# Attention in 64x64 tiles: the masked quadrant of the scores left out, the keys' halves swapped for half of the heads, and a tile's work in an order with two changes of tiling

## The chip, the cores and the metric

The kernel runs on one core of a Trainium2 chip. The metric is the device time of one execution in microseconds (us). The kernel before takes 419.59 us (median of three runs, 418.76 to 420.72).

The engines are named as the profile names them: PE is TensorE (PEld its weight loads), DVE is VectorE, ACT is ScalarE, POOL is GpSimd, SP is SyncE, which here only issues transfers. Each engine works through its own instructions in order. A matmul of 32-bit floats is one instruction in the program and two in the trace ("x16" in a row of the trace is eight in the code).

## What is computed

A linear attention with decay over 2 batches, 8 heads, 768 positions and 64 numbers a head, and behind it two layers of a mixture of experts with one expert a row (1536 rows of 512, 8 experts, hidden size 1024):

```python
for t in range(S):
    state = gamma[None, :, None, None] * state + np.einsum('bhd,bhe->bhde', k[:, :, t], v[:, :, t])
    y[:, :, t] = scale * np.einsum('bhd,bhde->bhe', q[:, :, t], state)
x = np.ascontiguousarray(attn_out.transpose(0, 2, 1, 3)).reshape(B * S, H * D)
x = _moe_ref(x=x, **moe_kwargs)      # out[mask] = gate_w * (relu(xe @ w1[e]) @ w2[e])
return _moe2_ref(x=x, **moe2_kwargs) # the same with a capacity of 384 rows an expert
```

The change touches only the attention and what follows it up to the rows and gate logits of its 12 tiles.

## The kernel before

The attention (lines 476 to 733) goes over 12 tiles of 128 positions, n = 2 c + b for chunk c of batch b, one tile in one turn of the loop at line 662. Inside a tile the recurrence is written as matmuls, with all 8 heads in two halves j and four pairs p:

- `a_load` (485): SP issues the tile's q, k (both transposed) and v with k by rows, 1 MB, three tiles ahead.
- `a_decay` (498): POOL multiplies v by the decay, giving `vp`, one tile ahead.
- `a_scores` (506): PE forms `sc`, keys by queries, 128 by 128 for each head with 64 rows of the array (the profile's 64\*128 tiling: two matmuls lie side by side); DVE multiplies by the causal mask into `Am` (515), one instruction for each half of the heads.
- `a_state` (518): PE forms `du`, the tile's addition to the state (128\*64 tiling), DVE adds it to the state (`wn`, 532), POOL decays it (`wm`, 534). The last two tiles have none.
- `a_past` (538): PE starts the output `ot` with the old state times q (64\*64 tiling: four matmuls side by side).
- `a_out` (551): PE adds `vp` times `Am` to `ot` (128\*64 tiling); DVE scales it into `xt` (562), one instruction for each half of the heads.
- `a_comb` (574, with `combine`, 1347): PE turns `xt` back to rows and forms the gate logits in one go, `cb` (128\*128 tiling); DVE sums the logits (`lgb`, 1358, or into `row` from tile 8 on), then ACT copies the rows out of PSUM (1363), for tiles 0 to 7 the logits too (1367), and issues the store of the rows to DRAM, `x1d` (569).

The order is written out by hand (`manual_schedule`), and a turn stands on PE as: scores of n, `cb` of n-2, past of n-1, state of n, out of n-1. That makes four changes of tiling a turn. The PSUM buffers of all these are five of one tag (`mmtile`), and `cb` has one of its own.

Between the tiles stands the routing of rows to experts: tiles 0 to 3 and 4 to 7 are routed as batches (`batch`, 582: pick, count at n = 5 and 9; rank, slots, place at n = 6 to 8 and 10), tiles 8 to 11 one by one (`route_tile`, 196: pick, rank, place). At n = 6 `choose` (387) picks the expert that goes first and at n = 10 `early` (419) starts the gather of its rows. At n = 0 ACT makes the matrices `iw` from the identity and the gate's weights (692, 693), at n = 10 it casts two of the first weights (`split_hi`, 158, line 163). The tail behind the loop (711 to 740) does the last tile in two halves, `ca` and `cb` of `Halves` (1371), with the routing of tiles 9 to 11 between them, and then the first products of layer 1 begin.

Of the kernel before, what the change touches and what calls it, by code (L numbers as in the profile page):

```python
# [10 lines left out]
F32 = mybir.dt.float32  # L11
# [7 lines left out]
P = 128  # L19
B, H, S, HD = 2, 8, 768, 64  # L20
# [23 lines left out]
_C = {}  # L44


def _consts(capacity):
# [10 lines left out]
    put("mask", (s[:, None] <= s[None, :]))  # L58
    put("dec", gamma[None, :] ** (127.0 - s[:, None]))
    hh = np.array([[2 * p + j for p in range(NP)] for j in range(2)]).repeat(HD, axis=0)  # L60
# [22 lines left out]
def fused(ctx, tc, qT, kT, vkr, wg, w11, w12, w21, w22, cst, out, capacity):  # L83
# [12 lines left out]
    def mmtile(name):  # L96
        return pp.tile([P, 512], F32, tag="mm", name=name, bufs=5)

    cs = cp.tile([P, cst.shape[1]], F32, name="cs")
    c0, c1 = _C["g128"][1], _C["ident"][1]  # L100

    def con(name):
        lo, hi = _C[name]
        return cs[:, lo:hi]

# [369 lines left out]
    over = cp.tile([P, 2], F32, name="over")  # L475
    with tc.tile_pool(name="ap", bufs=3) as ap:
        W = []
        for b in range(B):
# [19 lines left out]
        def a_decay(n):  # L498
            if n >= NT:
                return  # L500
            vp = ap.tile([P, H, HD], F32, tag="vp", name="vp", bufs=3)
            dlo, dhi = _C["dec"]
            (V if n == 1 else G).tensor_mul(vp, ld[n][3], cs[:, dlo:dhi].unsqueeze(2).to_broadcast([P, H, HD]))
            vps[n] = vp

        def a_scores(n):
            qb, kt, k_, v_ = ld[n]
            Am = ap.tile([P, NP, 2, P], F32, tag="Am", name="Am", bufs=2)
            sc = [mmtile("sc").rearrange("p (a t) -> p a t", t=P) for _ in range(2)]
            for p in range(NP):  # L510
                for j in range(2):
                    hs = slice(j * HD, (j + 1) * HD)
                    T.matmul(sc[j][:, p, :], kt[hs, p, :], qb[hs, p, :], start=True, stop=True)  # L513
            for j in range(2):
                V.tensor_mul(Am[:, :, j, :], sc[j], con("mask").unsqueeze(1).to_broadcast([P, NP, P]))
            st_[n] = (vps.pop(n), Am)
# [33 lines left out]

        def a_out(n, beside=None):
            c, b = divmod(n, B)
            vp, Am = st_.pop(n)
            ot = st_.pop(("o", n))
            xt = ap.tile([P, NP, P], F32, tag="xt", name="xt", bufs=2)
            for j in range(2):
                for a in range(2):
                    for u in range(2):
                        p = 2 * a + u
                        T.matmul(ot[j][u * HD:(u + 1) * HD, a, :], vp[:, 2 * p + j, :], Am[:, p, j, :], start=not c,  # L560
                                 stop=True, skip_group_check=True)
                V.tensor_mul(xt[:, 2 * j:2 * j + 2], ot[j],
                             con("g").rearrange("p (k t) -> p k t", k=KD)[:, 2 * j:2 * j + 2])
                if beside is not None:
                    beside(j, xt[:, 2 * j:2 * j + 2])
            st_[("x", n)] = xt

        def a_store(n, row, cols=slice(0, RW)):
            nc.scalar.dma_start(x1d[n * P:(n + 1) * P, cols], row[:, cols])

        tlo, _ = _C["tok"]
        lgb = ap.tile([P, nb, E], F32, name="lgb", bufs=1)

        def a_comb(n):
            row, lg = combine(nc, pp, rp, st_.pop(("x", n)), iw[0], None, P, lgb[:, n, :] if n < nb else None)
            a_store(n, row)
            return lg

        def a_route(n, lg):
            return route_tile(rt1, lg, cs[:, tlo + n:tlo + n + 1], None, P, n == NT - 1, None, ("place",))  # L580

        def batch(at, lo, hi):
# [23 lines left out]
            def rank():  # L606
# [9 lines left out]
                V.tensor_mul(rt1["E"][:, lo:hi, :], oh, cs[:, tlo + lo:tlo + hi].unsqueeze(2).to_broadcast(sh))  # L616
                ro = small("ro")
# [24 lines left out]
        a_load(0)  # L642
        nc.sync.dma_start(cs[:, :c0], cst[:, :c0])
        a_load(1)
        nc.sync.dma_start(cs[:, c0:c1], cst[:, c0:c1])
        nc.scalar.dma_start(wgs, wg)
# [3 lines left out]
        def step(n, i):  # L650
            if n in steps:
                steps[n][i]()
# [8 lines left out]
        a_decay(0)  # L661
        for n in range(NT):
            a_scores(n)
            a_decay(n + 1)
            comb(n - 2)
            if n:
                a_past(n - 1)
            step(n - 3, 1)
            if n == first + 1:
                many[0][2]()  # L670
            if n == first + 1:
                know_first = choose(rt1, 0, run[:, 1, :])
            if n == second + 1:
                many[1][2]()
                many[1][3](4)
# [14 lines left out]
            if n == 0:  # L690
                for i in range(2):
                    A.copy(iw[i][:, :, 0:P], ident.unsqueeze(1).to_broadcast([P, KD, P]))
                    A.copy(iw[i][:, :, P:], wgs[:, i])
                nc.sync.dma_start(cs[:, c1:], cst[:, c1:])
            if n == 2:
# [17 lines left out]

        def beside(i, xt):
            if i == 0:
                step(NT - 3, 1)
                comb(NT - 2)
                step(NT - 2, 0)
            else:
                rt1["x"] = first_x(rt1["rows"])  # L720
                way.half(0, mmtile("ca"), last[0])
                a_store(NT - 1, way.row, slice(0, 2 * P))
                step(NT - 3, 2)
                step(NT - 2, 1)
                way.half(1, mmtile("cb"), xt)
            last.append(xt)

        last = []
        a_past(NT - 1)
        a_out(NT - 1, beside)  # L730
        a_store(NT - 1, way.row, slice(2 * P, RW))
# [552 lines left out]
    def dropped():  # L1284
# [6 lines left out]
                 "r": rp.tile([P, 1], F32, tag="dr", name="dr", bufs=1)}  # L1291
        tlo, _ = _C["tok"]
        for n in range(NT):
            b, c = divmod(n, NC)
            at = c * B + b
            tok = cs[:, tlo + at:tlo + at + 1]
            lg = rp.tile([P, E], F32, tag="dl", name="dl")
# [48 lines left out]

def combine(nc, pp, rp, xt, iw, gate, cnt, lg=None):
# [98 lines left out]
```

## Time and profile before

| | |
|---|---|
| median of three runs | 419.59 us |
| profiled execution | 420.54 us, of which 418.8 us from its first to its last instruction |
| PE busy over the span | 405.5 us (97%) |
| DVE, ACT, POOL busy | 76%, 57%, 24% |
| granted PE clock over the span | 0.998 |
| attention, from the first scores to the last half of the last tile | 4.65 to about 61 us |

PE is busy nearly all the time, in the attention too. A row of the chain of waits or of the timeline reads: start and length in us, engine, what it did, how many instructions are merged ("x16"); in brackets the idle time ahead of it and what ended that. Matmuls overlap, so the length of a merged row runs to the end of the last of them, while in the chain each piece runs to the start of the next.

### The profile page before, as it was taken

The numbers are of one execution on the slowest core, as the hardware profiler recorded it, in microseconds if no ns is written. First come the engines' busy times: TensorE is split into PE (matmuls) and PEld (weight loads), VectorE is DVE, ScalarE is ACT, GpSimd is POOL, SyncE is SP. The second block draws the span as 40 slices with busy tenths as digits, with TensorE's granted clock in tenths as the row PEclk, the third lists the DMA queues.
The fourth block names the chain that finished last, engine by engine and source line by source line (L and its number), as shares of the span: only waits on it lengthen the run. The fifth ranks groups of instructions, "written<-read, shape, count | busy, mean of one in ns | idle before, by whom it ended". The sixth has DMA issues, their size and how long they took to land.

```text
span 418.8 us, 9473 instructions
## 1 busy us (share of the span) xinstructions
PE 405.5 (97%) x3403; PEld 381.0 (91%) x3403; DVE 319.4 (76%) x885; ACT 238.8 (57%) x485; POOL 99.6 (24%) x104
## 2 busy tenths in 40 slices
PE   7999999999999999999999999999999999999993
PEld 6887789999999999999999998998888999999993
DVE  3677787788889898989798966478586788888840
ACT  2111232666766677767575622566676778788550
POOL 1443314105042332314001112003201404021021
PEclk9999999999999999999999999999999999999999
DMA  8998963876767767677757803778767777778611
GB/s 310 400 335 303 380 271 94 290 245 214 232 203 231 236 236 229 216 224 240 227 170 256 302 25 89 277 268 297 251 197 267 234 238 254 256 242 271 226 37 32
DMA packets 30630, 97.42 MB, mean 233 GB/s; under 512 B 4289, under 2 KB 4801, under 8 KB 30576
## 3 DMA queue, kind: packets, MB, share of 16 engines
q1 hardware_dynamic: 23760, 79.56, 56.6%
q0 software_dynamic: 4512, 13.17, 9.2%
q10 hardware_dynamic: 2304, 4.02, 2.5%
q8 instruction: 29, 0.48, 0.5%
q14 instruction: 25, 0.20, 0.2%
HBM read 87.03 MB, written 9.81 MB: 231 GB/s over the span
## 4 chain that ended last, share of the span: by engine, by line
PE 84%; DVE 7%; issue 3%; DMA 3%; ACT 1%; SPq 0%; POOL 0%; POOLq 0%; DVEq 0%; ACTq 0%
PE y L840 17%; PE h L796 16%; PE h L797 7%; PE y L841 7%; PE h L439 7%; PE cb L1352 6%; PE o L855 3%; PE o L857 3%; PE o L856 3%; PE tp L367 2%; PE sc L513 2%; DVE wlo L174 2%; PE ot L560 2%; DMA vk<-vkr 1%; PE ot L547 1%
## 5 line engine op out<-in xcount | busy, mean ns | idle before, releaser
L174 DVE TENSOR_TENSOR wlo<-st,whi 128x1024 fp32r<-128x1024 f32 x120 | 145.0, 1216 | 2.4 <-ACT whi L163 2.4
L163 ACT CAST whi<-st 128x1024 fp32r<-128x1024 f32 x120 | 124.9, 1045 | 20.0 <-DMA st<-w 19.3
L840 PE MATMUL y<-h,whi 128*128 128x416 f32 (+9 forms) x384 | 116.5, 369 | 0.1
L796 PE MATMUL h<-x,whi 128*128 128x416 f32 (+9 forms) x384 | 114.0, 365 | 0.0
L841 PE MATMUL y<-h,wlo 128*128 128x208 f32 (+9 forms) x384 | 96.3, 251 | 0.0
L797 PE MATMUL h<-x,wlo 128*128 128x208 f32 (+9 forms) x384 | 96.2, 250 | 0.0
L840 PEld LDWEIGHTS y<-h,whi 128*128 128x128 f32 x384 | 72.1, 188 | 2.4 <-DVE rro L236 0.5
L796 PEld LDWEIGHTS h<-x,whi 128*128 128x128 f32 x384 | 72.1, 188 | 1.8 <-issue 0.6
L797 PEld LDWEIGHTS h<-x,wlo 128*128 128x128 f32 x384 | 73.3, 191 | 0.1
L841 PEld LDWEIGHTS y<-h,wlo 128*128 128x128 f32 x384 | 73.3, 191 | 0.0
L325 POOL DMA_INDIRECT out<-ob,oi x14 | 15.0, 1072 | 111.4 <-ACT ob L868 94.6
L808 DVE SCALAR_TENSOR_TENSOR h<-hs,h 128x416 fp32r<-128x416 f32 (+9 forms) x48 | 26.9, 561 | 18.9 <-ACT h L807 16.7
L807 ACT ACTIVATE h<-hs 128x416 fp32r<-128x416 f32 (+9 forms) x48 | 25.1, 523 | 25.5 <-DVE hs L782 24.5
L1057 POOL DMA_DIRECT2D x2d<-row x16 | 9.3, 584 | 112.4 <-ACT h L807 96.7
L782 DVE TENSOR_TENSOR hs<-h,hb 128x208 f32<-128x208 f32 (+9 forms) x96 | 29.8, 348 | 6.3 <-ACT ob L868 4.0
L439 PE MATMUL h<-x,whole 128*128 128x128 f32 (+1 forms) x256 | 30.8, 278 | 0.7 <-ACT x L383 0.7
L781 ACT COPY hb<-h 128x208 f32<-128x208 f32 (+9 forms) x96 | 27.2, 318 | 7.0 <-PE h L797 6.0
L439 PEld LDWEIGHTS h<-x,whole 128*128 128x128 f32 x256 | 29.4, 192 | 1.3 <-ACT x L383 0.9
L1363 ACT COPY row<-cb 128x512 f32<-128x512 f32 x11 | 6.4, 586 | 39.4 <-DVE lgb L1358 29.4
L352 POOL DMA_INDIRECT rows<-x1d,igs x14 | 26.2, 1873 | 11.1 <-ACT gx L757 5.1
L782 DVE TENSOR_TENSOR yt<-y,yb 128x208 f32<-128x208 f32 (+9 forms) x48 | 15.0, 353 | 13.5 <-ACT yb L781 13.5
L855 PE MATMUL o<-whi,h 128*128 128x512 f32 (+1 forms) x64 | 24.2, 378 | 0.0
(198 smaller groups left out, 620.0 us busy)
## 6 DMA issues: line engine op xcount, KB each, us to landing
st<-w SPq DMA_DIRECT2D x120, 512.0 KB, 3.6
vk<-vkr SPq DMA_DIRECT2D x11, 512.0 KB, 6.3
whole<-w SPq DMA_DIRECT2D x8, 512.0 KB, 7.6
qb<-qT SPq DMA_DIRECT2D x12, 256.0 KB, 4.9
x1d<-row ACTq DMA_DIRECT2D x11, 260.0 KB, 6.1
kt<-kT SPq DMA_DIRECT2D x11, 256.0 KB, 5.4
x2d<-row POOLq DMA_DIRECT2D x8, 260.5 KB
vk<-vkr ACTq DMA_DIRECT2D x1, 512.0 KB, 4.6
```

The costliest lines, as they stand in the source:

```text
L163: A.copy(hi, st)
L174: V.tensor_sub(lo, st, hi)
L352: ins = nc.gpsimd.indirect_dma_start(t, None, xd[0:n, :], bass.IndirectOffsetOnAxis(ap=index, axis=0), bounds_check=n - 1, oob_is_err=Fals ...
L439: T.matmul(ps[:, j], w[:, k, j % 2 * P:(j % 2 + 1) * P], x[:, k], start=k == 0, stop=k == KD - 1, skip_group_check=True)
L781: A.copy(b, ps[:, 1, :])
L782: V.tensor_add(out, ps[:, 0, :], b)
L796: T.matmul(ps, hi[:, k, fs], x[:, k, :, :cap], start=k == 0, stop=False, skip_group_check=True)
L797: T.matmul(ps[:, 0, :], lo[:, k, fs], x[:, k, 0, :cap], start=False, stop=k == KD - 1, skip_group_check=True)
L808: V.scalar_tensor_tensor(h[:, sl, 1, :cap], s, 0.0, h[:, sl, 0, :cap], ALU.max, ALU.subtract)
L840: T.matmul(ps[i], hi[:, ds], h[:, f, :, :cap], start=f == 0, stop=False, skip_group_check=True)
L841: T.matmul(ps[i][:, 0, :], lo[:, ds], h[:, f, 0, :cap], start=False, stop=f == KF - 1, skip_group_check=True)
L855: T.matmul(p, h[:, f, 0, ts_], hi, start=f == 0, stop=False)
```

## The change

The 128 by 128 scores of a head have a quadrant that the mask sets to zero: late keys against early queries. It is left out. The scores are formed by matmuls of 64 keys, in 64\*64 tiling: early keys against all 128 queries, late keys against the late queries. `Am` is 3 blocks of 64 columns a head, not 128 twice, so that the mask multiplication has 384 columns in place of 512. For the second half of the heads (v = 1, heads 4 to 7) early and late keys change places on the partitions; the host swaps the rows of v and k to match (`rows`, `dec` and the mask follow).

The output is built from three parts: the old state as before (`a_past`); `a_near`, the near diagonal blocks by 64\*64 matmuls in two steps (`same` is True where the row group of the array and the PSUM bank of the output belong together, False where they are crossed); `a_far`, both halves of the keys against the late queries (128\*64). Between the two steps of `a_near` ACT copies one number out of `ot` (`fence`, line 577 of the changed kernel), which the second step waits for. `combine` in the attention writes 64 rows at a time (128\*64 tiling, as `a_far` and `a_state` have it).

A turn on PE is now: past of n-1, near True of n-1, scores of n, near False of n-1, far of n-1, state of n, `cb` of n-2. `a_turned` is what DVE did in `a_out`. The constants for the attention alone move into the attention's own pool (`ca`), and the identity comes by a transfer of its own. In the tail the last tile is done whole before the rows of tile 10.

```diff
+    put("mask", np.block([[tri, full, tri], [tri, tri, full]]))
+    put("dec", gamma[None, :] ** (127.0 - np.where(np.arange(H)[None, :] < H // 2, s[:, None], (s[:, None] + HD) % P)))
...
         def a_scores(n):
             qb, kt, k_, v_ = ld[n]
-            Am = ap.tile([P, NP, 2, P], F32, tag="Am", name="Am", bufs=2)
-            sc = [mmtile("sc").rearrange("p (a t) -> p a t", t=P) for _ in range(2)]
-            for p in range(NP):
-                for j in range(2):
-                    hs = slice(j * HD, (j + 1) * HD)
-                    T.matmul(sc[j][:, p, :], kt[hs, p, :], qb[hs, p, :], start=True, stop=True)
-            for j in range(2):
-                V.tensor_mul(Am[:, :, j, :], sc[j], con("mask").unsqueeze(1).to_broadcast([P, NP, P]))
+            Am = ap.tile([P, 2, 2, 3, HD], F32, tag="Am", name="Am", bufs=2)
+            sc = [mmtile("sc")[:, 0:6 * HD].rearrange("p (u k t) -> p u k t", u=2, k=3) for _ in range(2)]
+            lo, hi = slice(0, HD), slice(HD, P)
+
+            def one(r, u, v, late):
+                p, hs = 2 * v + u, slice(r * HD, (r + 1) * HD)
+                at = (hi, lo)[v] if late else (lo, hi)[v]
+                ks = 1 + v if late else slice(0, 2 + v, 1 + v)
+                T.matmul(sc[r][at, u, ks, :], kt[hs, p, hi if late else lo], qb[hs, p, hi] if late else qb[hs, p, :],
+                         start=True, stop=True)
+
+            for late in (False, True):
+                for u in range(2):
+                    for r, v in ((0, 0), (1, 1), (0, 1), (1, 0)):
+                        one(r, u, v, late)
...
+        def a_near(n, same):
...
+            for u in range(2):
+                for r in (range(2) if same else (1, 0)):
+                    v = r if same else 1 - r
+                    rs = slice(v * HD, (v + 1) * HD)
+                    T.matmul(ot[r][u * HD:(u + 1) * HD, v, 0:HD], vp[rs, 4 * v + 2 * u + r, :], Am[rs, r, u, 0, :],
+                             start=same and not c, stop=False, skip_group_check=True)
+            if same:
+                A.copy(rp.tile([P, 1], F32, tag="fence", name="fence")[0:1], ot[1][0:1, 1, 0:1])
+
+        def a_far(n):
...
+                        T.matmul(ot[r][u * HD:(u + 1) * HD, v, HD:], vp[:, 4 * v + 2 * u + r, :], Am[:, r, u, 1 + v, :],
+                                 start=False, stop=True, skip_group_check=True)
...
         for n in range(NT):
+            if n:
+                a_past(n - 1)
+                a_near(n - 1, True)
             a_scores(n)
             a_decay(n + 1)
+            if n:
+                a_near(n - 1, False)
+                a_far(n - 1)
+            if n == second + 1:
+                many[1][2]()
+                many[1][3](4)
+            if n:
+                a_turned(n - 1)
+            a_state(n)
             comb(n - 2)
-            if n:
-                a_past(n - 1)
             step(n - 3, 1)
...
-            a_state(n)
             if first < n < first + 3:
                 many[0][3](2)
-            if n:
-                a_out(n - 1)
...
     for k in range(KD):
         lo = (k % 2) * (P + E)
-        nc.tensor.matmul(cb[:, k // 2, lo:lo + P + E], xt[:, k, :], iw[:, k, :], start=True, stop=True)
+        for h in range(2 if apart_rows else 1):
+            rs = slice(h * HD, (h + 1) * HD) if apart_rows else slice(0, cnt)
+            nc.tensor.matmul(cb[rs, k // 2, lo:lo + P + E], xt[:, k, rs], iw[:, k, :], start=True, stop=True)
```

What stands in a row on PE in an ordinary turn, here that of tile 4, before (each row: line, operation, output and inputs, shape of the output, count; `wm` is the old state):

```order
L513 MATMUL sc<-qb,kt 128x128 x8
L1352 MATMUL cb<-iw_75,xt 128x136 x4
L547 MATMUL ot<-qb,wm_233 64x128 x8
L529 MATMUL du<-vp,vk 64x64 x8
L560 MATMUL ot<-Am,vp 64x128 x8
```

and after:

```order
L562 MATMUL ot<-qb,wm_272 64x128 x8
L574 MATMUL ot<-Am,vp 64x64 x4
L521 MATMUL sc<-qb,kt 64x128
L521 MATMUL sc<-qb,kt 64x2x64 x2
L521 MATMUL sc<-qb,kt 64x128 x2
L521 MATMUL sc<-qb,kt 64x2x64 x2
L521 MATMUL sc<-qb,kt 64x128
L521 MATMUL sc<-qb,kt 64x64 x8
L574 MATMUL ot<-Am,vp 64x64 x4
L585 MATMUL ot<-Am,vp 64x64 x8
L544 MATMUL du<-vp,vk 64x64 x8
L1385 MATMUL cb<-iw_75,xt 64x136 x8
```

All that has 64\*64 tiling stands together at the front (L562 to the second L574), all that has 128\*64 behind it, and `cb` has moved from second to last place in the turn. With the waits shown, the second step of `a_near` on PE is the one that waits for ACT:

```order
L521 MATMUL sc<-qb,kt 64x64 x8
L574 MATMUL ot<-Am,vp 64x64 [waits Activation_49]
L574 MATMUL ot<-Am,vp 64x64 x3
L585 MATMUL ot<-Am,vp 64x64 x8
```

Before, no matmul that adds to `ot` waited for ACT. On ACT an ordinary turn held the row copy, the copy of the logits and the issue of the store, before:

```order
L1363 COPY row<-cb 128x512 [waits DVE_49]
L1367 COPY row<-lgb 128x8
L569 DMA x1d<-row 128x520 [waits DMAHW3_49,Activation_49]
L1363 COPY row<-cb 128x512 [waits DVE_49]
```

and after:

```order
L1396 COPY row<-cb 128x512 [waits DVE_49]
L1400 COPY row<-lgb 128x8
L599 DMA x1d<-row 128x520 [waits DMAHW6_49,Activation_49]
L577 COPY fence<-ot 1x1 [waits PE_49]
L1396 COPY row<-cb 128x512 [waits DVE_49]
```

The fence of a turn now stands on ACT behind the row copy, the logits' copy and the store of the turn before. On ACT from turn 10 to turn 11, before (`st` are weights as loaded):

```order
L1363 COPY row<-cb 128x512 [waits DMAHW4_49,DVE_49]
L569 DMA x1d<-row 128x520 [waits DMAHW6_49,Activation_49]
L163 CAST whi<-st 128x1024 [waits DMAHW3_49]
L163 CAST whi<-st 128x1024 [waits DMAHW4_49]
L1363 COPY row<-cb 128x512 [waits DMAHW5_49,DVE_49]
```

and after:

```order
L1396 COPY row<-cb 128x512 [waits DMAHW7_49,DVE_49]
L599 DMA x1d<-row 128x520 [waits DMAHW1_49,Activation_49]
L167 CAST whi<-st 128x1024 [waits DMAHW4_49]
L167 CAST whi<-st 128x1024
L577 COPY fence<-ot 1x1 [waits PE_49]
```

The fence of turn 11 stands behind the two casts.

## Rows read from the trace of the kernel before

**Rows 1.** Chain of waits, one turn on PE and a later `du`: start, length, engine, what

```profile
18.09 0.62 PE du L529 x16
18.70 0.88 PE ot L560 x16
19.58 1.09 PE sc L513 x16
20.67 1.12 PE cb L1352 x8
21.79 0.60 PE ot L547 x16
...
45.44 0.61 PE du L529 x16
```

**Rows 2.** Timeline, from a `cb` in layer 1 to its logits, no change of tiling

```profile
93.07 1.10 PE L1352 MATMUL cb<-iw,yt 128*128 128x136 f32 x8
...
94.21 0.19 DVE L1358 TENSOR_REDUCE row<-cb 128x8 f32<-128x32 f32 x1 [0.18 <-PE cb L1352]
```

**Rows 3.** Timeline of PE, 21.70 to 21.74 us, at the start of a past

```profile
21.51 0.28 PE L1352 MATMUL cb<-iw,xt 128*128 128x136 f32 x1
21.72 0.33 PE L547 MATMUL ot<-qb,wm 64*64 64x128 f32 x3
```

**Rows 4.** Timeline, from a `cb` through DVE and ACT to the store

```profile
20.60 1.19 PE L1352 MATMUL cb<-iw,xt 128*128 128x136 f32 x8
...
21.91 0.18 DVE L1358 TENSOR_REDUCE lgb<-cb 128x8 f32<-128x32 f32 x1
22.12 0.59 ACT L1363 COPY row<-cb 128x512 f32<-128x512 f32 x1 [3.62 <-DVE lgb L1358]
...
22.83 0.36 ACTq L569 DMA_DIRECT2D x1d<-row  x1
```

**Rows 5.** Timeline, a store issued on ACT and the casts behind it

```profile
50.78 0.33 ACTq L569 DMA_DIRECT2D x1d<-row  x1
51.15 1.99 ACT L163 CAST whi<-st 128x1024 fp32r<-128x1024 f32 x2 [0.40 <-DMA whole<-w]
```

**Rows 6.** Timeline, what DVE does with `du` and `ot` in a turn

```profile
23.12 0.42 DVE L532 TENSOR_TENSOR wn<-du,wm 128x256 f32<-128x256 f32 x1 [1.04 <-PE du L529]
...
23.49 0.86 DVE L562 TENSOR_TENSOR xt<-ot,cs 128x256 f32<-128x256 f32 x2
```

**Rows 7.** Timeline, the last `iw` copy on ACT and two `vp` on POOL

```profile
10.78 0.21 ACT L693 COPY iw<-wgs 128x32 f32<-128x32 f32 x1
...
16.58 1.04 POOL L503 TENSOR_TENSOR vp<-vk,cs 128x512 f32<-128x512 f32 x1 [2.35 <-DMA vk<-vkr]
...
29.04 1.07 POOL L503 TENSOR_TENSOR vp<-vk,cs 128x512 f32<-128x512 f32 x1 [0.50 <-DMA vk<-vkr]
```

**Rows 8.** Timeline, DVE's list of routing and choice in turn 6

```profile
31.61 0.18 DVE L616 TENSOR_TENSOR E<-boh,cs 128x32 f16<-128x32 f16 x1
...
33.44 0.86 DVE L627 TENSOR_SCALAR bR<-iota,r 128x256 f16<-128x256 f16 x2
```

**Rows 9.** Timeline, DVE's lists in turns 9 to 11, and the last half

```profile
47.32 0.18 DVE L593 TENSOR_REDUCE bm<-lgb 128x4 f32<-128x32 f32 x1
...
48.76 1.28 DVE L515 TENSOR_TENSOR Am<-sc,cs 128x512 f32<-128x512 f32 x2
...
50.05 0.73 DVE L616 TENSOR_TENSOR E<-boh,cs 128x32 f16<-128x32 f16 x1
...
51.94 0.75 DVE L562 TENSOR_TENSOR xt<-ot,cs 128x256 f32<-128x256 f32 x2
...
55.60 0.18 DVE L1358 TENSOR_REDUCE row<-cb 128x8 f32<-128x32 f32 x1
...
56.10 0.29 DVE L238 TENSOR_SCALAR rR<-iota,r 128x256 f16<-128x256 f16 x1
...
60.69 0.73 PE L1383 MATMUL cb<-iw,xt 128*128 128x136 f32 x4
```

More of the change, by code (lines that the diff above doesn't have):

```diff
@@ L56, in put @@
         parts.append(a)
-    put("mask", (s[:, None] <= s[None, :]))
-    put("dec", gamma[None, :] ** (127.0 - s[:, None]))
+    half = np.arange(HD)
+    tri = (half[:, None] <= half[None, :])
+    full = np.ones((HD, HD))
+    put("mask", np.block([[tri, full, tri], [tri, tri, full]]))
+    put("dec", gamma[None, :] ** (127.0 - np.where(np.arange(H)[None, :] < H // 2, s[:, None], (s[:, None] + HD) % P)))
     hh = np.array([[2 * p + j for p in range(NP)] for j in range(2)]).repeat(HD, axis=0)
@@ L97, in mmtile @@
         return pp.tile([P, 512], F32, tag="mm", name=name, bufs=5)
-    cs = cp.tile([P, cst.shape[1]], F32, name="cs")
-    c0, c1 = _C["g128"][1], _C["ident"][1]
+    c0, c1, c2 = _C["g128"][1], _C["g"][1], _C["ident"][1]
+    cs = cp.tile([P, cst.shape[1] - c1], F32, name="cs")
+    first_cs = []
     def con(name):
         lo, hi = _C[name]
-        return cs[:, lo:hi]
+        return first_cs[0][:, lo:hi] if hi <= c1 else cs[:, lo - c1:hi - c1]
     iw = [cp.tile([P, KD, P + E], F32, name=f"iw{i}") for i in range(2)]
@@ L476, in fused @@
     with tc.tile_pool(name="ap", bufs=3) as ap:
+        ca = ap.tile([P, c1], F32, name="ca", bufs=1)
+        first_cs.append(ca)
         W = []
@@ L554, in a_out, with a_turned @@
+        def a_far(n):
+            vp, Am = st_[n]
+            ot = st_[("o", n)]
+            for r in range(2):
+                for v in range(2):
+                    for u in range(2):
+                        T.matmul(ot[r][u * HD:(u + 1) * HD, v, HD:], vp[:, 4 * v + 2 * u + r, :], Am[:, r, u, 1 + v, :],
+                                 start=False, stop=True, skip_group_check=True)
+        def a_turned(n):
             ot = st_.pop(("o", n))
+            st_.pop(n)
             xt = ap.tile([P, NP, P], F32, tag="xt", name="xt", bufs=2)
@@ L556, in a_out @@
             for j in range(2):
[L557 to L561, printed above, removed]
                 V.tensor_mul(xt[:, 2 * j:2 * j + 2], ot[j],
                              con("g").rearrange("p (k t) -> p k t", k=KD)[:, 2 * j:2 * j + 2])
-                if beside is not None:
-                    beside(j, xt[:, 2 * j:2 * j + 2])
@@ L566, in a_out @@
             st_[("x", n)] = xt
+            return xt
         def a_store(n, row, cols=slice(0, RW)):
             nc.scalar.dma_start(x1d[n * P:(n + 1) * P, cols], row[:, cols])
-        tlo, _ = _C["tok"]
+        tok = con("tok")
         lgb = ap.tile([P, nb, E], F32, name="lgb", bufs=1)
         def a_comb(n):
-            row, lg = combine(nc, pp, rp, st_.pop(("x", n)), iw[0], None, P, lgb[:, n, :] if n < nb else None)
+            row, lg = combine(nc, pp, rp, st_.pop(("x", n)), iw[0], None, P, lgb[:, n, :] if n < nb else None, True)
@@ L712, in fused @@
         way = Halves(nc, rp, iw[0], None, P)
[L714 to L728, printed above, removed]
-        a_past(NT - 1)
-        a_out(NT - 1, beside)
+        a_past(NT - 1)
+        a_near(NT - 1, True)
+        a_far(NT - 1)
+        a_near(NT - 1, False)
+        xt = a_turned(NT - 1)
+        step(NT - 3, 1)
+        comb(NT - 2)
+        step(NT - 2, 0)
+        rt1["x"] = first_x(rt1["rows"])
+        way.half(0, mmtile("ca"), xt[:, 0:2])
+        a_store(NT - 1, way.row, slice(0, 2 * P))
+        step(NT - 3, 2)
+        step(NT - 2, 1)
+        way.half(1, mmtile("cb"), xt[:, 2:4])
         a_store(NT - 1, way.row, slice(2 * P, RW))
```

34 lines of the change are left out of this document (17 added, 17 removed).

## The prediction

> **What bounds the kernel now.** I read the page's table of busy shares first, then the chain of waits over the attention, then the timeline of one turn. In the chain a turn is PE alone: state, out, scores, `cb`, past, 0.62 + 0.88 + 1.09 + 1.12 + 0.60 = 4.31 us [rows 1]. DVE has 1.28 + 0.86 + 0.42 + 0.18 = 2.74 us of work in it [rows 4, 6, 9]; ACT and POOL have less. What is to be seen in rows 4 is a second path, today without price: `cb` starts, DVE sums its logits 1.31 us later, ACT copies the rows 0.21 later, issues the store 0.71 after that and stands in the issue for 0.36. Nothing on PE waits for its end.
>
> The durations come from the profiled execution of 420.54 us. 1.7 us of it lie outside the span and stay. The median is 0.95 lower; I put the difference that I find on the median. A change of 0.5%, 2.1 us, is about what a measurement can tell from none.
>
> **PE's own work in a turn.** From rows 1 the price of a pass (half a 32-bit matmul): out follows state with no change of tiling, 16 passes in 0.88, two side by side, so a round of 128 columns takes 0.11. A `cb` pass of 136 columns, alone, takes (1.10 - 0.28) / 7 = 0.117 in layer 1 [rows 2]; the 0.28 is the length of one alone, the last of a `cb` [rows 3]. Eight are 0.94, so the change ahead of them costs 1.12 - 0.94 = 0.18. Past has 16 passes in 0.60, less 0.18 about 0.44: four rounds of 0.11, four side by side. State: 64 columns, (0.62 - 0.18) / 8 = 0.055 a round of two. Four changes of tiling cost some 0.7 us a turn.
>
> The new turn: past 0.44; near True, eight passes of 64 columns in two rounds of four, 0.11; scores, 16 passes of 128 columns (0.44) and 16 of 64 (0.22), four side by side, 0.66 in place of 1.09; near False 0.11; far 0.45; state 0.45; `cb` in 16 passes two side by side, 8 x 0.117 = 0.94 as before; two changes 0.36. Sum 3.52 us, 0.79 less than now. If PE alone set the turn, that would be the gain.
>
> The Trainium skill, "TensorE: Matmul & The Clock Gate", section "Wait — 56ns, not 53.3ns?", says that starts are never less than about 25 ns apart, however few columns. By it the 32 short passes of scores and near would take 0.80, not 0.44, and the turn 3.88. The trace does not agree: a window that ends 0.02 us after a past begins holds three starts [rows 3]. I keep 3.52 for PE; by the figure of the Trainium skill the sum below would hardly move, but the fast rival would fall.
>
> **The wait that takes its place.** The second step of near waits for the fence, and the fence is behind the row copy and the store on ACT. So the second path of rows 4 now comes back to PE. From the start of `cb`: logits at 1.14, since no change of tiling stands ahead of it now (93.07 to 94.21 [rows 2]); row copy 0.21 later, store 0.71 after that (22.12 to 22.83 [rows 4]); ACT's next instruction 0.37 behind the store (50.78 to 51.15 [rows 5]; the profile puts that idle time down to a transfer, but it is the length of the issue); the fence, which the trace does not show, 0.21 as the smallest copy on ACT [rows 7], bounds 0.21 and the 0.59 of the 512-column copy from PSUM [rows 4]: I take the lower end, since it copies one number; 0.03 to restart PE, as from the logits' end to the row copy [rows 4]. Sum 2.67. PE alone would be there at 0.94 + 0.18 + 0.44 + 0.11 + 0.66 = 2.33, so it waits 0.34 a turn. Behind the wait are queued near False, change, far, state and the next `cb`: 2.67 + 0.11 + 0.18 + 0.45 + 0.45 = **3.86 us a turn** in place of 4.31. Of the 0.79 that PE gains, 0.45 is left.
>
> DVE fits, barely: `Am` shrinks with its columns to 1.28 x 384 / 512 = 0.96 (bounds 0.96 and 1.28), runs from 2.5 to 3.5, `xt` after far from 3.6 to 4.46, `wn` to 4.88, the next logits are due at 3.86 + 1.14 = 5.00. Loads don't bind: the tiles that POOL waits for land (29.04 - 16.58) / 4 = 3.1 us apart [rows 7], under 3.86. POOL has 1.7 us of work a turn; the smaller transfers of constants move nothing.
>
> **The start.** The first fence stands on ACT behind the `iw` copies, which end at 10.99 [rows 7]. So near False of tile 0 starts at 11.26, and then far, state, near, scores, near, far, state with two more changes bring `cb` of tile 0 to 14.6, one turn later state of tile 3 to 18.0. It is at 18.09 now [rows 1]. -0.1 us: out of tile 0 is over a microsecond later than now, and the shorter turns give that back.
>
> **Turns 3 to 9.** From state of tile 3 to state of tile 9 it takes 45.44 - 18.09 = 27.35 now [rows 1]. Six turns of 3.86 are 23.2. DVE's list in turn 6, from 31.61 to 34.30 less the 0.42 of a `wn` in it [rows 6, 8], 2.27 us, starts behind the logits at 1.32; `Am`, `xt`, `wn` behind it end at 5.83 and the logits, due at 5.00, come 0.8 late. That delay goes through ACT and the fence to PE in full. 24.0 in all: -3.3 us.
>
> **Turn 9 to the last half.** It is 60.69 - 45.44 = 15.25 now [rows 1, 9]. After, from the start of `cb` of tile 7: logits done 1.32, DVE's pick list 1.44 (47.32 to 48.76), `Am` 0.96, then from E to the end of `xt` 2.64 (50.05 to 52.69) [rows 9]: 6.36. Logits 0.18 and 0.03, row copy from 6.57, store 0.61 behind its start (0.59 and 0.02), ACT free of it 0.37 later at 7.55, and then the two casts, 1.99 [rows 5], to 9.54: the fence of turn 11 is behind them and PE goes on at 9.8. Without the casts it would be 7.8. Today they cost nothing, because nothing on PE waits behind them. From 9.8: near False and far to 10.56, logits of tile 9 at 11.70, DVE to the end of rR 0.79 (55.60 to 56.39 [rows 9]), placing 0.3 (estimate), past and near 0.55, change and far 0.63, change and near False 0.29, ranks 0.3, change and `cb` of tile 10 1.12, change and four transposes 0.65, the first half 0.47, 0.1 more: 16.9. With the 0.45 from state to `cb` 17.35: +2.1 us.
>
> **Sum:** -0.1 - 3.3 + 2.1 = -1.3 us. What follows the attention is the same in both and moves with it. 419.59 - 1.3 = **418.3 us**, no change that a measurement would tell for sure. Every 0.1 in the turn is worth 0.8 us (one turn at the start, six, one at the end); lists and tail may be off by 1: own range 416.8 to 420.0.
>
> **The rivals.** *The fence is hidden.* Should the issue of the store not hold ACT, or the copies come sooner, PE's own 3.52 sets the turn: 6 x 0.34 = 2.0 more, and 0 to 2.0 more where the casts don't hold the fence: 414.3 to 416.3, about 415.3. For it: 0.34 is a small gap between two sums of many terms. Against it: rows 5. By the 25 ns of the Trainium skill it could not happen.
>
> *Slower: a longer trip through ACT.* A fence of 0.59 makes the turn 4.24, and an `Am` that stays at 1.28 makes DVE late by another 0.1 a turn: 4.35, +0.49 x 8 = 3.9, 422.2. It decides from a turn of 4.29 on, where 421.7 is reached. For it: one read of PSUM right behind a matmul is in no row; against it: the copies' cost falls with their size.
>
> *The change doesn't do what it says:* four matmuls don't run side by side in the new order of scores, which goes through the four corners diagonally, nor in near. Then each of them takes two rounds for one, 0.66 + 0.22 more, PE's turn is 4.40, over the trip by 0.54: + 4.3, 422.6. Slower from the same 4.29. Against it: past does run four at a time.
>
> **How the numbers follow.** Forecast 0.57, hidden fence 0.20, longer trip 0.13, not side by side 0.08, anything else 0.02. Faster than 417.5: the hidden fence and a fifth of the forecast, 0.31. Slower than 421.7: two thirds of the longer trip, the next, the rest, 0.19. Within: 0.50. The range goes from the middle of the hidden fence to where the slower cases begin, 415.2 to 421.8.
>
> **What would show it.** Right: PE waits for ACT's fence in nearly every turn, 0.2 to 0.5 us each and some 2 us in turn 11; turns near 3.9 us in the chain, with copies, store and fence in it; scores at 0.66 between past and near; only two gaps of a change. Wrong: no wait at the second near and turns near 3.5 (the fence is hidden); fence rows of 0.4 or more; matmuls of scores starting two at a time; POOL waiting for loads in turns 4 to 8, which I leave out; a turn 11 without the stall.

## The result, and the profile after

The changed kernel takes 425.39 us (median, 424.73 to 426.01) against 419.77 us for the kernel before on the same chip: a ratio of 1.0134, 95% interval 1.0103 to 1.0165. It is 5.6 us slower, where no change was forecast. Its profiled execution, at 426.01 us the longest of the four, has a span of 424.2 us at a granted clock of 0.998. The other three had 0.987 to 0.992 and took less time, so the profiled one is not slow for its clock; how the time of the other three divides between the clock and what follows, no trace shows.

What PE waited for up to the end of the attention, by what ended the wait (engine and operation, "<-" releaser, us in total, times, the longest). After:

```profile
PE ot L574 <- ACT fence L577: 5.2, 6, 2.2
PE sc L521 <- issue: 3.2, 2, 2.0
PE du L544 <- issue: 1.8, 1, 1.8
...
PE ot L562 <- issue: 0.5, 1, 0.5
```

The first line was predicted: the second step of near waits for the fence. The lines with "issue" were not: 5.5 us in which PE waited for no semaphore. In the same view of before there is no such line. They are four pieces, each in the middle of a run of matmuls on one tile. The timeline of PE shows them, and beside them the cast and the fence of turn 11:

```profile
17.35 0.34 PE L574 MATMUL ot<-Am,vp 64*64 64x64 f32 x8 [0.17 <-ACT fence L577]
...
20.23 0.57 PE L544 MATMUL du<-vp,vk 128*64 128x64 f32 x13 [1.81 <-issue]
...
30.66 0.56 PE L562 MATMUL ot<-qb,wm 64*64 64x128 f32 x12 [0.52 <-issue]
...
45.05 0.67 PE L521 MATMUL sc<-qb,kt 64*64 64x128 f32 x22 [1.18 <-issue]
...
51.10 0.34 PE L521 MATMUL sc<-qb,kt 64*64 64x64 f32 x8 [1.99 <-issue]
...
55.63 1.99 ACT L167 CAST whi<-st 128x1024 fp32r<-128x1024 f32 x2 [0.40 <-ACT row L1396]
...
57.52 0.14 ACT L577 COPY fence<-ot 1x1 f32<-1x1 f32 x1
57.72 0.34 PE L574 MATMUL ot<-Am,vp 64*64 64x64 f32 x8 [1.95 <-ACT fence L577]
...
64.95 0.71 PE L1416 MATMUL cb<-iw,xt 128*128 128x136 f32 x4
```

The last row is the last half of the last tile, at 60.69 before [rows 9]: 4.26 later. The chain of waits for one turn, to be read against [rows 1]; the turn is the fence's trip, as forecast, and then 1.81 us of nothing:

```profile
14.81 1.00 PE cb L1385 x16
...
15.83 0.20 DVE lgb L1391
...
16.06 0.02 ACT row L1396
16.08 0.46 issue
16.54 0.21 ACT row L1400
16.77 0.34 ACTq L599
...
17.15 0.16 ACT fence L577
...
17.35 0.34 PE ot L574 x8
17.69 0.61 PE ot L585 x16
18.31 0.11 PE du L544 x3
18.42 1.81 issue
20.23 0.57 PE du L544 x13
20.80 0.95 PE cb L1385 x16
```

The page gives two more numbers, PE's instructions (3403 before) and the queues that bring instructions to the engines (29 packets on q8 before):

```profile
PE 402.9 (95%) x3875; PEld 379.6 (90%) x3875; DVE 315.7 (74%) x885; ACT 240.4 (57%) x497; POOL 98.5 (23%) x104
...
q8 instruction: 32, 0.52, 0.5%
```

A packet on q8 has 16 KB (0.52 MB / 32). I counted all of PE's rows in the trace in order of start, from zero: 3875 weight loads, as many matmuls and 69 rows of its sequencer (waits on semaphores), 7819 in all, which is 30.5 times 256. Beside them I put the start of each 16 KB packet on q8. PE's stand-stills end at rows 705, 1217, 1985 and 2241, whole multiples of 256 rows apart. So the table goes by rows 256 apart: when PE entered the 256 rows ahead, when the packet between started, when this row started (in brackets a start held back by 0.2 while PE still worked):

```
after    row   entered  packet   starts  stand-still | before  row  entered  packet   starts
         705    13.83    18.05    20.23     1.81     |         449     9.72   13.22    18.08
         961    20.23    22.74    24.90    (0.2)     |         705    18.08   20.47    26.02
        1217    24.90    28.25    30.66     0.52     |         961    26.02   27.41    32.63
        1473    30.66    32.23    34.79      -       |        1217    32.63   33.55    41.18
        1729    34.79    36.13    38.73      -       |        1473    41.18   43.78    49.10
        1985    38.73    42.61    45.05     1.18     |        1729    49.10   51.57    57.77
        2241    45.05    48.68    51.10     1.99     |
```

Wherever PE stood still, its next instruction started 2.16 to 2.44 us after the packet did. Before, 4.86 us or more lay between; a block was there long before PE came to it, because 256 instructions lasted 6.6 to 8.7 us. In the new turn they last 3.9 to 4.1 where nothing is late. **Supply theory:** PE's instructions come in blocks of 256 (the distances of the stand-stills); the packet for the next one is asked for when PE enters a block, waits behind the loads on the DMA engines (1.3 to 4.2 us in the table), and PE stands still when it comes too late. The Trainium skill, "Runtime: NRT & Kernel Launch", section "Instruction fetch mechanics", says that instructions come in blocks of 16 KiB, 256 of them, over a DMA queue of the engine's own, and that the cost is mostly hidden. The trace agrees on the size (q8's packets); hidden the cost is in the kernel before, and not in this one. **Rival, mix theory:** the pieces belong to the new mix of matmuls in all four corners of the array, and the multiples of 256 are chance.

### The profile page after: what moved, and what is told of

The parts are those of the page before. It is cut to its first block, busy times and chain, and to the rows that moved or that the text cites. A ratio compares the mean times of both kernels' runs of the same rounds, so it can differ in the third digit from the quotient of the medians.

```text
span 424.2 us, 10440 instructions
## 1 busy us (share of the span) xinstructions
PE 402.9 (95%) x3875; PEld 379.6 (90%) x3875; DVE 315.7 (74%) x885; ACT 240.4 (57%) x497; POOL 98.5 (23%) x104
## 4 chain that ended last, share of the span: by engine, by line
PE 79%; DVE 7%; issue 5%; DMA 4%; ACT 3%; ACTq 0%; POOL 0%; POOLq 0%; SPq 0%; DVEq 0%
PE y L871 17%; PE h L827 16%; PE y L872 7%; PE h L828 7%; PE h L443 6%; PE cb L1385 5%; PE o L886 3%; PE o L887 3%; PE o L888 3%; PE tp L371 2%; DVE wlo L178 2%; PE ot L585 2%; DMA cs<-cst 1%; DMA st<-w 1%; PE du L544 1%
## 5 line engine op out<-in xcount | busy, mean ns | idle before, releaser
L443 PE MATMUL h<-x,whole 128*128 128x128 f32 (+1 forms) x256 | 30.5, 277 | 0.0
L356 POOL DMA_INDIRECT rows<-x1d,igs x14 | 24.5, 1749 | 9.5 <-ACT gx L788 4.6
L886 PE MATMUL o<-whi,h 128*128 128x512 f32 (+1 forms) x64 | 24.3, 380 | 0.0
```

The lines of the kernel that those rows point to most:

```text
L443: T.matmul(ps[:, j], w[:, k, j % 2 * P:(j % 2 + 1) * P], x[:, k], start=k == 0, stop=k == KD - 1, skip_group_check=True)
L886: T.matmul(p, h[:, f, 0, ts_], hi, start=f == 0, stop=False)
```

## Experiments

### The loads left out (a_few, b_few)

```diff
             if n >= NT:
+                return
+            if n > 2:
+                ld[n] = (kept[QM[n]][0], kept[KM[n]][1]) + kept[VM[n]][2:]
                 return
...
+            ld[n] = kept[n] = (qb, kt, k_, v_)
```

QM, KM and VM name which of tiles 0 to 2 stands in for a tile's q, k and v.

> The changed kernel, but only tiles 0 to 2 are loaded; tiles 3 to 11 use the q, k and v of these three again (9 MB of transfers left out; what is computed is another attention, as many instructions on every engine). Supply theory (PE's instructions come by DMA in blocks of 256, 16 KB each, and PE stands still in the middle of its stream when the block's transfer comes late behind the loads): the idle pieces called 'issue' on PE, 5.9 us up to 58 us in the changed kernel, fall to 1 us or less, the last half comes 4 to 6 us sooner, the time is 419.5 to 421.5. Rival, mix theory (the pieces belong to the new mix of matmuls on PE, 64 by 64 in all four corners, and not to any transfer): they stay, 425 plus or minus 1.

> The kernel before with the same 9 MB of transfers left out, as the control of a_few. Both theories: PE has next to no stand-still to lose, 418.5 to 420, within 1 us of the kernel before. The difference of a_few to b_few is then what the change is worth where loads don't disturb it: -1.3 us by the prediction, 0 to +2 if something beside the blocks was also missed.

a_few: 423.24 us, ratio to the kernel before 1.0079 (1.0048 to 1.0111). b_few: 419.43, ratio 0.9997 (0.9974 to 1.0019). PE's waits in a_few:

```profile
PE ot L580 <- ACT fence L583: 5.6, 7, 2.2
PE sc L527 <- issue: 1.4, 1, 1.4
```

and in the timeline:

```profile
48.08 0.27 PE L527 MATMUL sc<-qb,kt 64*64 64x64 f32 x2 [1.38 <-issue]
```

From 13 to 34 us hardly anything is loaded, and every stand-still there is gone. In three blocks the packet starts 0.2 to 0.3 us after PE enters the block (entered at 23.99, 28.83 and 33.22, packets at 24.28, 29.01 and 33.52), in the one ahead of them 1.2 us after it (19.55 and 20.75), and once 0.1 ahead of it (14.96 and 14.83), in b_few up to 0.6 ahead (25.46 and 24.83): what asks for a packet runs a little ahead of PE's rows. One stand-still is left, where the weights are loaded (packet 45.72, next instruction 48.08, 2.36 later). The mechanism holds; the time is above the 419.5 to 421.5 that I expected, since that one stayed and something was lost anew. With the fence ending the turn, it is now 3.91 us (fences end waits at 22.61 and 26.52), against 3.86 forecast. What was new is the clock (stretch, PE busy, PEld, DVE, ACT, POOL, granted clock, DMA share, GB/s):

```profile
12.00:13.00 1.00, 1.00 (x24) 0.88 (x24) 0.69 (x3) 0.00 (x0) 0.00 (x0) 0.50 0.30 99
```

PE had stood 2.19 us for the first fence; from 12 to 15 us its granted clock is 0.50, the 1.2 GHz level.

### By count or by place (a_shift)

```diff
+                if n == 1:
+                    for _ in range(32):
+                        T.matmul(warm[:, 0:HD], ones16, ones16[:, 0:HD], start=True, stop=True)
                 a_near(n - 1, False)
```

> The changed kernel with 32 small matmuls of ones (64 instructions of PE in the trace) put where PE waits for the first fence, 8.9 to 10.84 us. Their result is not used. Supply theory: the stand-stills of PE keep to every 256th instruction, so in the program they fall 64 instructions earlier: no longer behind the third pass of a du (18.42 us), the first of a past (30.13), the ninth and the 24th of a scores (43.87, 49.12), but, in order, inside scores, inside far or du, and so on; time within 1 us of the changed kernel, 424.5 to 426.5. Mix theory: they stay behind the same instructions.

426.22 us, 1.0149 (1.0124 to 1.0175). Its five longest stand-stills, in the timeline of PE:

```profile
14.14 0.61 PE L521 MATMUL sc<-qb,kt 64*64 64x128 f32 x18 [0.95 <-issue]
...
20.05 0.27 PE L521 MATMUL sc<-qb,kt 64*64 64x64 f32 x2 [1.74 <-issue]
...
29.61 0.62 PE L544 MATMUL du<-vp,vk 128*64 128x64 f32 x14 [0.62 <-issue]
...
50.72 0.39 PE L574 MATMUL ot<-Am,vp 64*64 64x64 f32 x5 [2.15 <-issue]
...
57.33 0.68 PE L521 MATMUL sc<-qb,kt 64*64 64x128 f32 x24 [0.51 <-issue]
```

They are ahead of rows 449, 705, 1217, 2241 and 2497. Three of these are the numbers of before, two are other multiples of 256 away (of 1985, 0.1 us is left), and all are now other instructions: scores where `du` was, `du` where past was. 64 harmless instructions ahead moved the places in the program, and the count stayed. The mix theory is out.

### Fewer loads on the way (a_paced, b_paced, a_paced4)

```diff
+    def paced(ins, wait=True):
+        if wait and len(went) >= 2 and len(went) < 42:
+            tc.add_manual_dep(ins, went[-2].name, mybir.DependencyInfo(
+                mybir.DependencyClass.Sync, mybir.DependencyReason.DATA), reason="few on the way")
+        went.append(ins)
...
-            nc.sync.dma_start(qb, qT[b, c])
+            paced(nc.sync.dma_start(qb, qT[b, c]).ins, n >= 3)
```

and so for the other loads; in a_paced4 the 2 is a 4 in both places.

> The changed kernel, but from tile 3 on each load of q, k, v or weights is issued only when the load before the last has landed, so that at most two (0.5 to 1 MB) are on the way instead of up to eight. Same transfers, same instructions on PE. Supply theory: the block's transfer now waits for fewer loads, 0.3 to 2 us after PE enters the block before instead of 1.2 to 4.2, so the stand-stills of 5.5 us fall to 2 or less: 421 to 423.5. What speaks against it: loads themselves may come later and POOL's vp wait for them. If the stand-stills belong to the program and not to the loads: 425.4 or more.

> The kernel before with the same pacing of loads as in a_paced, as its control. Supply theory: before has no stand-still at its block ends, nothing to gain: 419.6, or up to 1 us more where a later load makes POOL wait. If pacing gained here as much as in a_paced, it would be for another reason than PE's blocks.

> The pacing of a_paced, but with up to four loads on the way instead of two. Supply theory: the block's transfer waits longer than in a_paced and less than in the changed kernel; stand-stills of 2 to 4 us in place of 5.5, and the loads move at 300 to 400 GB/s instead of 240: between the changed kernel and some us more, 424 to 430. It beats the changed kernel only if four on the way suffice for the loads.

a_paced: 443.11 us, 1.0565 (1.053 to 1.06); b_paced: 439.06, 1.045 (1.0415 to 1.0486); a_paced4: 427.14, 1.016 (1.0098 to 1.0222). a_paced has no stand-still at a block's end:

```profile
PE ot L582 <- ACT fence L585: 11.0, 8, 3.2
PE du L552 <- POOL vp L516: 6.0, 5, 1.9
```

With two loads on the way they move at some 240 GB/s in place of 320 to 400, and now PE waits for the data: 17.7 us more to be rid of 5.5 (at a granted clock of 0.967), and 19.2 in the kernel before, which had nothing to be rid of. With four on the way, 3.8 us of stand-still are left of 5.5, and nothing is gained. The expected times of a_paced and b_paced failed, that of a_paced4 held. That the stand-stills go with the loads on the way is in part shown once more: from row 705 on packets start at most 2.0 us after PE enters a block, but most blocks also last longer (4.2 to 10.9 us), because PE waits for data.

a_late was to move the weights behind the tiles:

```diff
-            if n == first + 3:
+            if n == NT - 2:
                 for _ in range(4):
                     load_whole()
                 refill(2)
-            if n == NT - 2:
                 split_hi()
                 split_hi()
```

> The changed kernel with the six loads of weights of turn 8 (3 MB, 38 to 50 us) issued in turn 10 instead, from some 53 us on. Supply theory: the stand-stills at 43.87 (1.18 us) and 49.12 (1.99 us) fall under 0.3 us each, since no weights lie ahead of those blocks; a block around 55 to 60 may come late by up to 1 us instead; last half 2 to 3 us sooner, 422 to 423.5 if the weights still come in time for layer 1. Mix theory: the stand-stills stay, 425.4, or later where weights come late.

427.2 us, 1.0168 (1.0092 to 1.0245), above the 422 to 423.5 that I expected. It did not do what I wrote: SP has nothing else to wait for there and issued the four whole ones at 44.4 to 47.3 us, against 42.65 to 48.0. They are later by little and closer together, and the longest stand-still lies behind that burst (packet at 52.08, 5.3 us after PE entered the block):

```profile
54.52 0.34 PE L521 MATMUL sc<-qb,kt 64*64 64x64 f32 x8 [3.63 <-issue]
```

### The fence and the casts (a_dve, a_casts, a_paced_casts)

```diff
-                A.copy(rp.tile([P, 1], F32, tag="fence", name="fence")[0:1], ot[1][0:1, 1, 0:1])
+                V.tensor_copy(rp.tile([P, 1], F32, tag="fence", name="fence")[0:1], ot[1][0:1, 1, 0:1])
```

> The changed kernel with the fence copied by DVE instead of ACT, so that it is no longer behind the row copy, the store and the two casts. Fence alone (the trip of the prediction is what the turn waits for, the casts hold turn 11): the waits of 0.17 to 0.58 us a turn and the 1.95 of turn 11 go, -3 to -4, 421.5 to 422.5. Supply theory: PE comes to the ends of its blocks sooner and waits there longer, so that of the waits for the fence in turns 3 to 9 next to nothing is gained, and of turn 11 about half: -1 to -2, 423.5 to 424.5.

424.96 us, 1.0136 (1.0083 to 1.019): no different from the change itself, and above both expectations. PE's waits:

```profile
PE sc L521 <- issue: 2.4, 2, 2.0
PE ot L574 <- DVE fence L577: 2.1, 3, 0.9
PE du L544 <- issue: 2.0, 1, 2.0
PE ot L585 <- issue: 1.8, 2, 1.2
PE ot L562 <- issue: 1.2, 2, 0.9
```

The waits for the fence fell from 5.2 to 2.1 us, and the stand-stills rose from 5.5 to 7.4. PE comes sooner to the ends of its blocks and stands there. The casts the same way:

```diff
                 a_near(n - 1, False)
                 a_far(n - 1)
+            if n == NT - 1:
+                split_hi()
+                split_hi()
...
-            if n == NT - 2:
-                split_hi()
-                split_hi()
```

> The changed kernel with the two casts of weights on ACT put behind the fence of turn 11 instead of ahead of it. Prediction: the wait of 1.95 us at 57.72 falls away, -2.0, 423.4. Supply theory: PE then goes on at 55.8, but the block that ends 16 instructions later was asked for late (packet at 54.66, usable some 2.4 us behind that, 57.0), so that 1.1 us of it come back: -0.9, 424.5.

427.02 us, 1.0152 (1.0107 to 1.0197). The wait at turn 11 is gone (fence waits 2.3 us in all), the stand-stills are 9.4 us. They differed already ahead of the moved casts, so a single execution does not tell what the casts are worth here; both expected times failed.

> Both edits, few loads on the way and the casts behind the fence. Supply theory: with the stand-stills at 2 us or less and no casts in the way, what is left is the prediction's own sum without its 2.0 for the casts: 419.6 - 1.3 - 2.0 + 2 = 418.3, and 417 to 420.5 with pauses that also cost granted clock. If the stand-stills stay: 423.4.

442.98 us, 1.053 (1.0471 to 1.0589): as a_paced, held up by the loads, far above the expectation; it tells nothing on the casts.

### What is left without the loads (a_few_fill, a_few_fill_casts)

a_few with the edit of a_shift, and with that of a_casts on top.

> As a_few (tiles 3 to 11 use the data of tiles 0 to 2, 9 MB of transfers left out), and with the 32 small matmuls of a_shift where PE waits for the first fence, so that PE doesn't stand still there; their result is not used. Clock theory (what a_few lost beyond the prediction's terms is half the granted clock from 12 to 15 us, some 1.3 us, and one late block of 1.4): granted clock 1.00 there, 1 to 1.5 us less than a_few, 421.7 to 422.3. Rival (a further term of the prediction is wrong): 423.2 as a_few.

> As a_few_fill (same data left out), with the two casts of weights behind the fence of turn 11. Without loads in the way of PE's blocks there, the prediction's term for the casts should come in full: 2.0 less than a_few_fill, 419.7 to 420.3. Supply theory with weights still being loaded from 33 to 50 us: a late block may take up to 1 of it: 420 to 421.3. If the casts never were the bound: as a_few_fill.

a_few_fill: 422.55 us, 1.0057 (1.0034 to 1.0081); a_few_fill_casts: 421.07, 1.0017 (0.9993 to 1.0041). With PE kept busy, the granted clock stays at 1.00 from 9 to 20 us. Of a_few's 0.8% excess a quarter goes, less than expected and less than the noise can tell (the intervals overlap). Moving the casts took another 1.5 us between the medians, 0.4%, which is nearer to the prediction's 2.0, but the profiled execution of a_few_fill does not bear its reason out:

```profile
53.01 0.84 PE L527 MATMUL sc<-qb,kt 64*64 64x128 f32 x20 [1.43 <-issue]
53.56 0.14 ACT L583 COPY fence<-ot 1x1 f32<-1x1 f32 x1
```

A late block held the scores of turn 11 until after the casts, PE did not wait for the fence at all, and the granted clock behind it was 0.50 (54 to 56 us; 1.00 in a_few_fill_casts). So what the casts alone cost stays open. What then costs 0.2% more than b_few, which the noise doesn't tell from nothing, still holds late blocks:

```profile
PE ot L580 <- ACT fence L583: 2.4, 6, 0.9
PE sc L527 <- issue: 1.6, 2, 1.0
...
PE ot L580 <- issue: 0.4, 1, 0.4
```

### Instructions and parts (b_split, b_order, c_whole)

```diff
-                    T.matmul(sc[j][:, p, :], kt[hs, p, :], qb[hs, p, :], start=True, stop=True)
+                    for t in (slice(0, HD), slice(HD, P)):
+                        T.matmul(sc[j][:, p, t], kt[hs, p, :], qb[hs, p, t], start=True, stop=True)
```

and alike in past and out.

> The kernel before, with each matmul of scores, past and out cut into two of 64 columns: the same arithmetic, tilings, order and transfers, but 240 instructions of PE in a turn in the trace instead of 144. Supply theory: a block of 256 lasts 4.6 us instead of 7.7 when nothing is waited for, and while the loads run a block comes up to 6.4 us after the one before, so 'issue' pieces of 0.5 to 1.8 us appear at every 256th instruction, 4 to 9 us together, 424 to 429. Mix theory: no new corners, no new pieces: 419.6, up to 1 more for the added weight loads.

428.45 us, 1.0214 (1.0163 to 1.0264): the expected time for another reason. No piece is "issue"; the cut matmuls themselves are dearer. The chain, against [rows 1]:

```profile
16.46 1.98 PE sc L514 x32
...
19.57 0.69 PE ot L549 x30
...
20.87 0.98 PE ot L563 x32
```

Scores take 1.98 in place of 1.09, 0.062 us a pass against 0.068: here a pass with 128 columns of weights and 64 of data costs nearly what one with 128 of data costs. A block then lasts 5.6 us, and the packets came some 0.2 us in time (packet at 18.08, row 705 at 20.75, that is 2.67 us in between). So this run, meant to tell the theories apart, didn't.

b_order takes scores, past, out, state, `cb` in this order, with `cb` in 64 rows at a time, and nothing else of the change.

> The kernel before with only the order of a turn and the split of cb taken from the change: scores, past, out, state, cb with 64 rows at a time. No fence, no 64 by 64 scores, three changes of tiling a turn instead of four, 160 instructions of PE in a turn in the trace instead of 144. By the prices of the prediction the turn is 4.31 - 0.18 = 4.13, -1.8 us over ten turns: 417.9. Supply theory: a block of 256 then lasts 6.6 us, just over the 6.4 that a late block takes, so stand-stills of at most 0.3 us each: 417.5 to 419. Mix theory: the same, 417.9.

419.23 us, 0.9997 (0.9972 to 1.0022). PE's waits:

```profile
PE du L529 <- POOL vp L503: 1.8, 1, 1.8
PE tp L382 <- DMA rows<-x1d,eig: 1.8, 1, 1.8
```

The turn is 4.11 us in the chain (`cb` at 15.50 and at 19.61), 0.2 less, with no stand-still (a block lasts 6.5 us), and what it gains is lost at both ends: PE comes to `du` of tile 2 ahead of its load, and to the early rows ahead of their gather. That is just above the 417.5 to 419 that I expected.

c_whole keeps the new scores and gives DVE the work of near and far: `Am` is whole, its masked quadrant zeroed once, and out and the tail are those of before.

```diff
+                V.tensor_mul(Am[:, r, :, :, 1, :], sc[r][:, :, 1:3, :],
+                             mk[:, 1:3].unsqueeze(1).to_broadcast([P, 2, 2, HD]))
+                for v, hs in ((0, lo), (1, hi)):
+                    V.tensor_mul(Am[hs, r, :, v, 0, :], sc[r][hs, :, 0, :],
+                                 mk[hs, 0].unsqueeze(1).to_broadcast([HD, 2, HD]))
```

> The changed kernel's scores (64 by 64, masked quadrant left out, halves of the keys swapped) with the out of the kernel before: DVE writes the products into a whole 128 by 128 Am whose masked quadrant was set to zero once (six instructions a tile instead of two), out is one matmul a head over all 128 keys, no near, no far, no fence; the tail is that of before. 192 instructions of PE in a turn instead of 224 (before: 144). PE's own turn 3.73 us (past 0.44, scores 0.66, out 0.88, state 0.45, cb 0.94, two changes 0.36) against 4.31. Fence theory alone: no trip through ACT and no casts in the way, 10 x 0.58 = -5.8, DVE's longer lists +1: 415. Supply theory: a block of 256 lasts 4.97 us, and where loads run one comes only every 5 to 6.4: some 4 us of stand-still come back: 418 to 420.

425.11 us, 1.0142 (1.0111 to 1.0173), far above both expectations; the profiled execution is the fastest of the four, 422.45. PE's turn is 3.7 us where it waits for nothing (`cb` at 15.01 and 18.69), and two late blocks are left (0.60 and 0.81). But PE now waits for DVE, which has six instructions a tile for `Am`:

```profile
PE tbp L251 <- DVE rR L242: 2.0, 1, 2.0
...
PE ot L570 <- DVE Am L537: 1.7, 3, 0.9
PE brk L632 <- DVE boh L620: 1.6, 1, 1.6
```

None of these versions beats the kernel before.

## Why the prediction was wrong

**What bounds the kernel, and the wait that takes its place: right.** From the start of `cb` to the second near it is 17.35 - 14.81 = 2.54 us against 2.67 forecast; the fence itself 0.16 (0.21 forecast). The turn where nothing else interferes is 3.91 in a_few (3.86). PE's wait in it is only half of the forecast, 0.16 to 0.18 us in place of 0.34, since PE itself comes to it later; that the turn still came out is in part luck. The pieces of PE's own turn agree: far with its change 0.61 (0.63), `cb` 0.95 (0.94), and near:

```profile
48.45 0.11 PE ot L574 x8
48.56 0.55 PE sc L521 x24
```

0.014 us a pass. The 25 ns of the Trainium skill ("TensorE: Matmul & The Clock Gate", "Wait — 56ns, not 53.3ns?") were rightly not used; this row differs from them.

**The start** came out near the forecast, state of tile 3 at 18.31 (18.0), by two errors that cancel: the first fence ended earlier, at 10.84 (11.26), and from there to `cb` of tile 0 it took 3.97 us (14.81 - 10.84), not 3.3.

**Turns 3 to 9** is the step that failed. I put 24.0 us, 3.3 less than before; from 18.31 to the state of tile 9 at 46.46 it took 28.15. In it lie stand-stills of 1.81, 0.52 and 1.18 and a `cb` of 1.28 for 0.95, broken at row 961, 3.84 in all. Without them it is 24.3: the sum of that step was right within 0.3 us, and a term was missing, the supply of PE's instructions, which I had put at nothing. "PE's own work in a turn" priced passes and changes of tiling, and never counted that a turn has 224 instructions in place of 144, to be brought in less time over the same DMA engines. The page had the number needed: 16 KB packets on q8, with PE's count beside them; and the DMA row stood near 400 GB/s. I took account of loads only as something that POOL waits for.

**Turn 9 to the last half:** 64.95 - 46.46 = 18.49 us against 17.35, one stand-still of 1.99 in it, of which some hides behind DVE's lists. The fence behind the casts held turn 11 for 1.95 (2.0 forecast).

**The sum.** +0.2 at the start, +0.8, +3.2: 4.26 us later at the last half. The first `y` starts 3.60 later (82.84, before 79.24), and the span is 5.4 longer. So the routing gives 0.7 back, and 1.8 us more are lost in the two layers, spread thinly; "what follows is the same" was wrong by that, and its cause stays open.

**The rivals.** The hidden fence: made by a_dve, and worth nothing while PE stands still at its blocks. The longer trip: no, the fence takes 0.16. Not side by side: no, the first 24 passes of scores, 16 of 128 columns and 8 of 64, take 0.55 us in the chain above (0.44 + 0.11 forecast). None of the rivals on the slower side, which had a chance of 0.19 together, was the one that came, and the time lies above the range.

**How much is shown.** That PE stands still at every 256th instruction when the packet is late is shown by a_shift (count, not place), a_few and, in part, a_paced (gone without loads in the way). How much of the 5.6 us it makes up is not measured: the stand-stills add up to 5.5, but they also hide other waits, as a_dve showed, only 3.6 us of delay are left at the first `y`, and a_few took away 4.1 us of stand-still and gained 2.2 (a stretch at half the granted clock came with it). Without loads and casts in the way the change costs 0.2% over the control, not told from nothing, still with 2.0 us of late blocks; forecast without the casts was a gain of 3.3, so that some 2 us remain unexplained (3.3 - 2.0 + 0.8). A part lies in the start: state of tile 3 comes at 19.36 there and at 17.44 in b_few, since the first fence, behind the `iw` copies, lets PE go on only at 11.03, and a late block of 0.95 follows at 14.22.

## What to carry to other kernels

Count instructions as you count microseconds: before cutting an engine's work into smaller pieces, divide 256 by its instructions per microsecond and compare that with what a block needs beside the loads (in the changed kernel up to 4.2 us until its packet starts and 2.4 more). In these profiles, "issue" in the middle of a run of equal matmuls, at distances of 256 instructions, meant that the engine lacked instructions. A shorter wait elsewhere bought nothing there (a_dve); fewer loads at that time took all but one of the stand-stills away (a_few), and with fewer instructions in a turn there were fewer of them (two late blocks in c_whole with 192, none in the kernel before with 144).

## What the runs showed of the hardware

- The packet with PE's next 256 instructions started 0.2 to 0.3 us after PE entered the block before in three blocks of a_few with few loads, up to 4.2 us after it in the changed kernel beside loads of 300 to 400 GB/s, and 5.3 after it in a_late; where PE had stood still, it went on 2.2 to 2.4 us after the packet's start.
- Half the columns of data did not halve a matmul's time where its weights have 128 columns (b_split): scores went from 1.09 to 1.98 us for twice the instructions with half the data each.
- A wait of PE of 2.2 us was followed by some 3 us at the 1.2 GHz level in a_few, and not in the profiled execution of the changed kernel, where the same wait was as long (10.84) and the clock 1.00 from 9 to 18 us.
